# Seven block products for eight in the first product of a two-layer feed-forward kernel's second layer

## The chip, the cores and the metric

The kernel runs on one core of one Trainium2 chip, as one launch. The metric is device time in microseconds (us) of that launch. Runs of a kernel are compared by their median; a profiled execution gives a trace of every instruction on TensorE (PE; its weight loads are PEld), VectorE (DVE), ScalarE (ACT), GpSimd (POOL) and the DMA queues.

## What is computed

```python
def reference(x, filt_r, filt_i, moe_w_in, moe_w_out, moe2_w_in, moe2_w_out):
    y = irfft(rfft(x, axis=1) * (filt_r + 1j * filt_i))   # x: (2, 3008, 256) float32
    t = y.reshape(6016, 256)
    h = t @ moe_w_in                                      # (256, 2048), float64 in memory
    t = where(h > 0, h, exp(min(h, 0)) - 1) @ moe_w_out   # (2048, 256)
    h = t @ moe2_w_in
    return (h * clip(h + 3, 0, 6) / 6) @ moe2_w_out
```

A long convolution along the sequence, then two feed-forward layers, each 256 to 2048 to 256 with a nonlinearity between its two products.

## The kernel before

The convolution is done as small Fourier matrices on TensorE; it fills the first part of the launch and is interleaved with layer one. The 6016 tokens lie in 12 blocks (`BLOCKS`: 512, 512, 512, 512, 480, 480 for each half of the batch), channels on partitions, tokens along the free dimension. The 2048 inner features are 16 chunks (`NF`) of 128.

Float32 is kept by splitting every operand in a high and a low float32r part (`split`, lines 74 to 76: ScalarE rounds a copy, VectorE subtracts it) and doing three matmuls for each product (`mm3`, lines 78 to 81: high by low, low by high, high by high).

A unit `u = (layer, block, chunk)` is one chunk of inner features for one block of tokens. `g1(u)` (line 328) does its first product: two halves of 128 input channels, so six matmuls into one PSUM bank. Then the nonlinearity: in layer one ScalarE's two activations and VectorE's combination (lines 341 to 345); in layer two ScalarE's ReLU with a bias of three and VectorE's minimum-and-multiply from the same bank (lines 347 to 350). `g_split(u)` splits the result, and `g2(u)` (line 359) does the second product, another six matmuls, summed over the 16 chunks in two PSUM banks (`outs`), which are emptied at a block's last chunk. Of 8 PSUM banks the other six go round among the `g1` results.

The program's order is written out by hand (`tc.manual_schedule()`), and each engine takes its instructions in that order. At step n (lines 587 to 596) come the functions listed in `pre[n]`, then `g1` of unit n, `g_split` of unit n-1, `g2` of unit n-3 (`SKEW`), then `post[n]`. So on VectorE the order at a step is: what `pre[n]` asks of it, the combination of unit n, the low half of the split of unit n-1; and the first matmul of `g2` reads that low half two steps later. Units 0 to 191 are layer one, 192 to 383 layer two, block after block.

Layer two's weights are float64 words in memory. During units 100 to 179 `w_chain` (line 291) makes the two float32r parts of each of the 16 chunks, seven small steps for each chunk, 112 steps dealt out over 80 units: `w_words` (VectorE and ScalarE), then `w_parts` (line 273), whose last step (line 283) ends a chunk and writes it to the scratch `scrw` by SyncE's queue (line 287). Odd chunks end at units 110, 120, ..., 170 and 179. The parts are read back by GpSimd's queue (`w_load`, line 314) into the buffers of layer one's weights as these come free, from unit 179 on. Layer one's outputs stay in SBUF (`x2`, line 387) and are split for layer two by `x_split`.

Three pools matter: `p4` has 20 buffers of 4 KB per partition (tag `t4`), `p2` 20 buffers of 2 KB (tag `t2`), `ps` the 8 PSUM banks. A new tile of a tag takes the buffer that came free first in program order and waits until its last user is done.

Of the kernel before, what the change touches and what calls it, by code (L numbers as in the profile page):

```python
# [13 lines left out]
ALU = mybir.AluOpType  # L14
# [23 lines left out]
def _f32(t):  # L38
    return t.bitcast(F32)
# [3 lines left out]
def fft_conv_moe_moe2(ctx, tc, xp, fq, sg, cs1, cs1t, cs2, ci2, ci1, ident, w1i, w1o, w2i, w2o, out):  # L43
# [34 lines left out]
    def mm3(acc, wh, wl, xh, xl, start, stop):  # L78
        nc.tensor.matmul(acc, wh, xl, start=start, stop=False)  # L79
        nc.tensor.matmul(acc, wl, xh, start=False, stop=False)  # L80
        nc.tensor.matmul(acc, wh, xh, start=False, stop=stop)  # L81
# [236 lines left out]
    xs, x2, gs, outs = {}, {}, {}, {}  # L318

    def x_split(layer, blk, h):  # L320
        n = BLOCKS[blk % 6]
        src = yblk[blk // 6, blk % 6] if layer == 0 else x2[blk]
        if h == 0:
            xs[layer, blk] = t4([P, 2, 512], F32R), t4([P, 2, 512], F32R)
        hi, lo = xs[layer, blk]
        split(hi[:, h, :n], lo[:, h, :n], src[:, h, :n])

    def g1(u):
        l, blk, f = u
# [10 lines left out]
        if l == 0:  # L340
            nc.scalar.activation(r[:, :n], acc[:, :n], AF.Relu, scale=-1.0)  # L341
            nc.scalar.activation(r[:, :n], r[:, :n], AF.Exp, scale=-1.0)  # L342
            nc.vector.scalar_tensor_tensor(  # L343
                out=r[:, :n], in0=r[:, :n], scalar=-1.0, in1=acc[:, :n], op0=ALU.add, op1=ALU.max
            )
        else:
            nc.scalar.activation(r[:, :n], acc[:, :n], AF.Relu, bias=three)  # L347
            nc.vector.scalar_tensor_tensor(  # L348
                out=r[:, :n], in0=r[:, :n], scalar=6.0, in1=acc[:, :n], op0=ALU.min, op1=ALU.mult
            )  # L350
        gs[u] = r

    def g_split(u):
        n = BLOCKS[u[1] % 6]
        gh, gl = t2([P, 512], F32R), t2([P, 512], F32R)
        split(gh[:, :n], gl[:, :n], gs[u][:, :n])
        gs[u] = gh, gl

    def g2(u):
        l, blk, f = u  # L360
        n = BLOCKS[blk % 6]
        gh, gl = gs.pop(u)
# [10 lines left out]
        sc = 1.0 if l == 0 else 1.0 / 6.0  # L373
        t0 = (blk // 6) * S + EDGES[blk % 6]
        dst = out[:, t0 : t0 + n].rearrange("(c p) t -> p c t", p=P)
        nc.scalar.activation(t[:, 0, :n], o[0][:, :n], AF.Copy, scale=sc)
        if u == units[-1]:
            m = n // 2
            nc.sync.dma_start(dst[:, 0, :], t[:, 0, :n])
            nc.scalar.activation(t[:, 1, :m], o[1][:, :m], AF.Copy, scale=sc)  # L380
            nc.vector.tensor_scalar_mul(t[:, 1, m:n], o[1][:, m:n], sc)
            nc.sync.dma_start(dst[:, 1, :], t[:, 1, :n])
            return
        nc.vector.tensor_scalar_mul(t[:, 1, :n], o[1][:, :n], sc)
        del outs[l, blk]
        if l == 0:
            x2[blk] = t
        else:
            nc.sync.dma_start(dst, t[:, :, :n])
# [9 lines left out]
    def at(slots, n, fn, *args):  # L399
        slots[n].append(lambda: fn(*args))  # L400
# [116 lines left out]
    with tc.manual_schedule():  # L517
        for key, src in (("s1t", cs1t), ("id", ident), ("sg", sg), ("s2", cs2), ("i2", ci2), ("i1", ci1)):
            load_mat(key, src)
        three = const.tile([P, 1], F32, name="three")  # L520
        nc.vector.memset(three, 3.0)
        engs = (nc.scalar, nc.vector)

        warm = const.tile([P, 512], F32, name="warm")
        nc.gpsimd.memset(warm, 0.0)
        acc = bank()
        for _ in range(WARM):
            nc.tensor.matmul(acc, warm[:, :P], warm, start=True, stop=True)
# [12 lines left out]
        nsign = 2  # L541
        for step in PROLOGUE.split():
            what, h, g = step[:-2], int(step[-2]), int(step[-1])
            if what == "T":
                tr(0, h, g, nc.scalar if g > 1 else engs[g])
            elif what == "S":
                s2_mm(0, h, g)
                mult(0, h, g)
            elif what == "A":
                s1t(0, h, g, engs[g % 2])  # L550
            elif what == "I":
                i2_mm(0, h, g)
# [129 lines left out]
```

## Time and profile before

| | |
|---|---|
| median of 3 runs (lowest to highest) | 1156.41 us (1154.66 to 1157.22) |
| the profiled execution's own time | 1154.02 us |
| its span, first to last instruction | 1152.3 us |
| PE busy | 1136.1 us |
| DVE busy | 760.1 us |
| ACT busy | 695.7 us |
| POOL busy | 73.7 us |

Matmuls are pipelined and the profile models their ends, so a matmul's duration is longer than the distance from its start to the next one's start. The rate of TensorE is read from starts. ACT and DVE instructions overlap a little too: two in a row start closer together than one lasts.

### The profile page before, as it was taken

Reading aid. Unit: us, or ns where it says so; the run is one execution under the profiler, and the core shown is the slowest. Engines: PE = TensorE matmul, PEld = TensorE weight load, DVE = VectorE, ACT = ScalarE, POOL = GpSimd, SP = SyncE. Lnnn points to the kernel's source line nnn. Section 1 sums busy time; section 2 is a strip of 40 time slices with the busy share of each in tenths; the row PEclk is TensorE's granted clock in tenths of the full one; section 3 lists DMA queues with packets and bytes.
Section 4 is the critical chain, followed back from the end, with each engine's and each line's share of the span. In section 5 each row is a group of like instructions: output and inputs, shape, how many; then the busy total and the mean of one; then the engine's idle time right before and its main releaser. Section 6 shows DMA issues by size and latency. Waiting matters only on the chain.

```text
span 1152.3 us, 13760 instructions
## 1 busy us (share of the span) xinstructions
PE 1136.1 (99%) x5212; PEld 942.7 (82%) x5212; DVE 760.1 (66%) x1206; ACT 695.7 (60%) x1237; POOL 73.7 (6%) x69
## 2 busy tenths in 40 slices
PE   8899999999999999999999999999999999999998
PEld 5588888788788888888888888888888888888887
DVE  6989998679963788787875555455455555455553
ACT  3477777876676777777776444444444444444443
POOL 3600000024310000000002000000000000000000
PEclk9999999999999999999999999999999999999999
DMA  9991100354522122222226100000000000000000
GB/s 290 290 300 65 42 1 1 110 160 148 165 74 72 37 74 73 74 74 73 81 84 202 54 19 1 19 19 1 19 18 1 18 19 1 19 19 1 19 18 18
DMA packets 50019, 79.75 MB, mean 69 GB/s; under 512 B 4000, under 2 KB 32544, under 8 KB 49952
## 3 DMA queue, kind: packets, MB, share of 16 engines
q1 hardware_dynamic: 46672, 70.14, 19.1%
q0 software_dynamic: 2304, 8.39, 2.4%
q8 instruction: 41, 0.67, 0.2%
q10 hardware_dynamic: 976, 0.34, 0.1%
q14 instruction: 26, 0.21, 0.1%
HBM read 54.87 MB, written 23.99 MB: 68 GB/s over the span
## 4 chain that ended last, share of the span: by engine, by line
PE 92%; DMA 4%; DVE 2%; ACT 0%; SPq 0%; issue 0%; POOL 0%; ACTq 0%; POOLq 0%; DVEq 0%
PE ps L79 30%; PE ps L81 30%; PE ps L80 30%; PE ps L216 2%; DMA raw<-in_w1o 1%; DMA t<-in_fq 1%; DMA t<-in_xp 1%; DVE t L190 1%; DVE t L189 1%; DMA id<-in_ident 1%; POOL t L192 0%; DVE t L76 0%; DMA t<-scr 0%; PE ps L197 0%; ACT t L75 0%
## 5 line engine op out<-in xcount | busy, mean ns | idle before, releaser
L79 PE MATMUL ps<-t,w 128*128 128x512 f32 (+1 forms) x1536 | 593.6, 386 | 0.6 <-DVE t L76 0.5
L81 PE MATMUL ps<-t,w 128*128 128x512 f32 (+1 forms) x1536 | 592.2, 386 | 0.0
L80 PE MATMUL ps<-t,w 128*128 128x512 f32 (+1 forms) x1536 | 592.1, 385 | 0.0
L76 DVE TENSOR_TENSOR t<-t,t 128x512 fp32r<-128x512 f32 (+2 forms) x472 | 329.0, 705 | 9.5 <-ACT t L75 7.6
L79 PEld LDWEIGHTS ps<-t,w 128*128 128x128 f32 x1536 | 288.2, 188 | 56.9 <-PE ps L81 0.9
L81 PEld LDWEIGHTS ps<-t,w 128*128 128x128 f32 x1536 | 288.2, 188 | 55.2
L80 PEld LDWEIGHTS ps<-t,w 128*128 128x128 f32 x1536 | 288.2, 188 | 54.8
L75 ACT ACTIVATE t<-t 128x512 fp32r<-128x512 f32 (+2 forms) x472 | 283.1, 611 | 24.6 <-POOL t L192 24.1
L348 DVE SCALAR_TENSOR_TENSOR t<-t,ps 128x512 f32<-128x512 f32 (+1 forms) x192 | 130.0, 677 | 250.7 <-ACT t L347 250.7
L347 ACT ACTIVATE t<-ps,three 128x512 f32<-128x512 f32 (+1 forms) x192 | 130.6, 680 | 268.6 <-PE ps L81 268.6
L343 DVE SCALAR_TENSOR_TENSOR t<-t,ps 128x512 f32<-128x512 f32 (+1 forms) x192 | 129.5, 675 | 109.3 <-ACT t L342 108.1
L341 ACT ACTIVATE t<-ps 128x512 f32<-128x512 f32 (+1 forms) x192 | 112.3, 585 | 104.5 <-PE ps L81 104.4
L342 ACT ACTIVATE t<-t 128x512 f32<-128x512 f32 (+1 forms) x192 | 119.8, 624 | 6.1
L125 POOL TENSOR_TENSOR t<-t,sg 128x512 f32<-128x512 f32 x24 | 30.3, 1265 | 191.6 <-DMA t<-in_fq 180.7
L192 POOL TENSOR_TENSOR t<-t,t 128x512 f32<-128x512 f32 x24 | 34.9, 1454 | 73.5 <-DVE t L190 48.8
L189 DVE TENSOR_TENSOR t<-ps,t 64x512 f32<-64x512 f32 x48 | 33.1, 689 | 5.7 <-POOL t L125 2.8
L216 PEld LDWEIGHTS ps<-i,t 96*128 96x128 f32 x256 | 31.3, 192 | 3.6 <-issue 2.5
L216 PE MATMUL ps<-i,t 96*128 96x94 f32 x256 | 31.1, 273 | 0.4 <-DMA t<-scr 0.4
L316 POOL DMA_DIRECT2D w<-scrw x16 | 8.6, 540 | 298.8 <-PE ps L81 298.8
L70 ACT ACTIVATE t<-ps 128x512 f32<-128x512 f32 (+12 forms) x51 | 19.4, 421 | 12.4 <-PE ps L149 8.0
L269 DVE SCALAR_TENSOR_TENSOR t<-raw,t 128x512 f32<-128x512 uint32 x32 | 22.3, 697 | 2.0
L263 DVE SCALAR_TENSOR_TENSOR t<-raw,t 128x512 uint32<-128x512 uint32 x32 | 22.7, 710 | 0.4
(54 smaller groups left out, 384.1 us busy)
## 6 DMA issues: line engine op xcount, KB each, us to landing
t<-in_fq SPq DMA_DIRECT2D x24, 512.0 KB, 6.2
scrw<-t SPq DMA_DIRECT2D x16, 512.0 KB, 3.0
w<-scrw POOLq DMA_DIRECT2D x16, 512.0 KB, 4.5
t<-in_xp SPq DMA_DIRECT2D x16, 384.0 KB, 5.2
scr<-t SPq DMA_DIRECT2D x24, 256.0 KB, 2.7
t<-scr SPq DMA_DIRECT2D x16, 384.0 KB, 5.1
raw<-in_w1i SPq DMA_DIRECT2D x18, 256.0 KB, 5.8
raw<-in_w1o SPq DMA_DIRECT2D x18, 256.0 KB, 5.7
```

The lines of the kernel that those rows point to most:

```text
L75: nc.scalar.activation(hi, src, AF.Copy)
L76: nc.vector.tensor_tensor(out=lo, in0=src, in1=_f32(hi), op=ALU.subtract)
L79: nc.tensor.matmul(acc, wh, xl, start=start, stop=False)
L80: nc.tensor.matmul(acc, wl, xh, start=False, stop=False)
L81: nc.tensor.matmul(acc, wh, xh, start=False, stop=stop)
L189: nc.vector.tensor_tensor(out=v[o], in0=acc[a], in1=flat(f[a, 1]), op=ALU.mult)
L216: nc.tensor.matmul(accs[h, jg][:, (j - jg * TG) * TJ : (j - jg * TG + 1) * TJ], vin[b, h, j // 8][:, j % 8, :], mats["i1"], start=True, st ...
L341: nc.scalar.activation(r[:, :n], acc[:, :n], AF.Relu, scale=-1.0)
L342: nc.scalar.activation(r[:, :n], r[:, :n], AF.Exp, scale=-1.0)
L343: nc.vector.scalar_tensor_tensor(out=r[:, :n], in0=r[:, :n], scalar=-1.0, in1=acc[:, :n], op0=ALU.add, op1=ALU.max)
L347: nc.scalar.activation(r[:, :n], acc[:, :n], AF.Relu, bias=three)
L348: nc.vector.scalar_tensor_tensor(out=r[:, :n], in0=r[:, :n], scalar=6.0, in1=acc[:, :n], op0=ALU.min, op1=ALU.mult)
```

## The change

In layer two the first product is done for pairs: two chunks of inner features by two blocks of tokens, with the 256 input channels as two halves, is a 2 by 2 by 2 product of blocks, done with seven block products and sums (Winograd's form of Strassen's scheme). Six pairs of blocks by eight pairs of chunks are 48 groups (`group(p, q, old, first)`).

- For each pair of chunks four weight sums are made (`w_sums`), split, written to the scratch `scrs` and read back (`s_load`): four GpSimd operations of 128x256, one ScalarE rounding of 128x512, one GpSimd subtraction of 128x512, one VectorE addition of 128x512. `w_sums` stands in the last step of `w_parts` for odd chunks.
- Layer one's outputs go to memory (`scrx`) and are read back per pair (`x2_load`, SyncE's queue); GpSimd makes four sums of them (`x_sums`), and seven operands are split (`x_part`) in place of four.
- In a group ScalarE copies three partial products out of PSUM (`copy`) and VectorE makes three sums (`add`); the fourth partial product builds up in its bank. The second product is the same as before, for four (chunk, block) pairs of the group before (`old`), its matmuls set between the seven products (`second` is `g2`'s inner part; 24 matmuls a group). ReLU and the gate read SBUF for three of the four.
- The outputs of both blocks of a pair take four PSUM banks, emptied in the next pair's first group (`out_evac`).
- The operands of the next pair are loaded, summed and split after groups q = 2 to 7 of each pair (`ahead2`); those of the first pair at units 160 to 188.

The diff, cut to its core (`copy`, `relu`, `gate` and `second` are as `copy` of a bank to SBUF, lines 347, 348 and 369 of before):

```diff
--- before.py
+++ after.py
@@ w_parts, layer two
             nc.sync.dma_start(scrw[f], _f32(hl.rearrange("p q f -> p (q f)")))
+            halves[f] = hl
+            if f % 2:
+                w_sums(f // 2)
         yield
+    def w_sums(q):
+        e, o = (_f32(halves.pop(f)) for f in (2 * q, 2 * q + 1))
+        a11, a12, a21, a22 = e[:, :, 0:P], e[:, :, P : 2 * P], o[:, :, 0:P], o[:, :, P : 2 * P]
+        t, r = t4([P, 2, 4, P]), t4([P, 2, 4, P], F32R)
+        s1, s2, s3, s4 = (t[:, :, i, :] for i in range(4))
+        for out, a, b, op in (
+            (s1, a21, a22, ALU.add), (s2, s1, a11, ALU.subtract),
+            (s3, a11, a21, ALU.subtract), (s4, a12, s2, ALU.subtract),
+        ):
+            nc.gpsimd.tensor_tensor(out=out, in0=a, in1=b, op=op)
+        th, tl, rh, rl = (x.rearrange("p i f -> p (i f)") for x in (t[:, 0], t[:, 1], r[:, 0], r[:, 1]))
+        nc.scalar.activation(rh, th, AF.Copy)
+        nc.gpsimd.tensor_tensor(out=th, in0=th, in1=_f32(rh), op=ALU.subtract)
+        nc.vector.tensor_tensor(out=rl, in0=th, in1=tl, op=ALU.add)
+        nc.sync.dma_start(scrs[q], _f32(r.rearrange("p q i f -> p (q i f)")))
...
+    def s_load(q):
+        if q < 3:
+            if q == 0:
+                sums["z"] = p12.tile([P, 3, 2, 4, P], F32R, tag="zt", name=name("zt"))
+            sums[q] = sums["z"][:, q]
+        else:
+            sums[q] = t4([P, 2, 4, P], F32R)
+        nc.gpsimd.dma_start(sums[q].rearrange("p q i f -> p (q i f)"), scrs[q])
...
@@ g2, end of a block of layer one
+        nc.scalar.activation(t[:, 0, :n], o[0][:, :n], AF.Copy)
+        nc.vector.tensor_copy(t[:, 1, :n], o[1][:, :n])
+        del outs[l, blk]
+        nc.sync.dma_start(scrx[blk][:, :, :n], t[:, :, :n])
...
+    def x_sums(p, i):
+        n = BLOCKS[2 * p % 6]
+        if i == 0:
+            xt[p] = [t2([P, 512]) for _ in range(4)]
+        b11, b21 = (xb[p, 0][:, c, :n] for c in range(2))
+        b12, b22 = (xb[p, 1][:, c, :n] for c in range(2))
+        t1, t2_, t3, t4_ = (t[:, :n] for t in xt[p])
+        out, a, b = ((t1, b12, b11), (t2_, b22, t1), (t3, b22, b12), (t4_, b21, t2_))[i]
+        nc.gpsimd.tensor_tensor(out=out, in0=a, in1=b, op=ALU.subtract)
+
+    def x_part(p, m):
+        n = BLOCKS[2 * p % 6]
+        src = {
+            1: xb[p, 0][:, 0], 2: xb[p, 0][:, 1], 3: xb[p, 1][:, 1],
+            4: xt[p][3], 5: xt[p][0], 6: xt[p][1], 7: xt[p][2],
+        }[m][:, :n]
+        ops[p, m] = t4([P, 2, 512], F32R)
+        split(ops[p, m][:, 0, :n], ops[p, m][:, 1, :n], src)
+    def prod(p, q, m, acc, start):
+        n = BLOCKS[2 * p % 6]
+        if m in (1, 2):
+            w = wts[1, 2 * q][:, :, (m - 1) * P : m * P]
+        elif m == 4:
+            w = wts[1, 2 * q + 1][:, :, P : 2 * P]
+        else:
+            w = sums[q][:, :, {5: 0, 6: 1, 7: 2, 3: 3}[m], :]
+        x = ops[p, m]
+        mm3(acc[:, :n], w[:, 0], w[:, 1], x[:, 0, :n], x[:, 1, :n], start, True, True)
...
+    def out_evac(p, k):
+        for d in range(2):
+            o, t = outs.pop((p, k, d)), t2([P, 512])
+            if d == 0:
+                nc.scalar.activation(t[:, :n], o[:, :n], AF.Copy, scale=1.0 / 6.0)
+            else:
+                nc.vector.tensor_scalar_mul(t[:, :n], o[:, :n], 1.0 / 6.0)
+            nc.sync.dma_start(out[d * P : (d + 1) * P, t0 : t0 + n], t[:, :n])
+
...
+        def add(self, key, u, bank_):
+            n = self.n
+            self.h[key] = t2([P, 512])
+            nc.vector.tensor_tensor(out=self.h[key][:, :n], in0=bank_[:, :n], in1=u[:, :n], op=ALU.add)
+        def part(self, key):
+            n, g = self.n, self.g[key]
+            gh, gl = t2([P, 512], F32R), t2([P, 512], F32R)
+            split(gh[:, :n], gl[:, :n], g[:, :n])
+            self.g[key] = gh, gl
...
+    def group(p, q, old, first):
+        g = Group(p, q)
+        a, b, c = bank(), bank(), bank()
+        prod(p, q, 1, a, True)
+        m1 = g.copy(a)
+        prod(p, q, 2, b, True)
+        g.add((0, 0), m1, b)
+        if old:
+            old.part((1, 0))
+            old.relu((0, 1))
+            old.gate((0, 1))
+            old.second((0, 0))
+        else:
+            first[0]()
+        g.relu((0, 0))
+        if old:
+            old.part((0, 1))
+        g.gate((0, 0))
+        prod(p, q, 6, a, False)
+        u2 = g.copy(a)
+        prod(p, q, 5, c, True)
+        g.part((0, 0))
+        if old:
+            old.second((1, 1))
+        else:
+            first[1]()
+        prod(p, q, 7, a, False)
+        u3 = g.copy(a)
+        g.add((1, 1), u3, c)
+        if old:
+            old.second((1, 0))
+            if old.q == NF // 2 - 1:
+                out_evac(old.p, 0)
+        else:
+            first[2]()
+        g.relu((1, 1))
+        g.gate((1, 1))
+        if old:
+            old.second((0, 1), (0,))
+        prod(p, q, 4, a, False)
+        g.h[1, 0] = a
+        g.relu((1, 0))
+        g.gate((1, 0))
+        if old:
+            old.second((0, 1), (1,))
+            if old.q == NF // 2 - 1:
+                out_evac(old.p, 1)
+        g.part((1, 1))
+        prod(p, q, 3, c, False)
+        g.add((0, 1), u2, c)
+        return g
...
-    units += [(1, blk, f) for blk in range(12) for f in range(NF)]
+    for q in range(NF // 2):
+        at(post, 172 + q, s_load, q)
+    for n, fn, i in ((160, x2_load, 0), (161, x2_load, 1), (166, x_sums, 0), (167, x_sums, 1), (168, x_sums, 2),
+                     (169, x_sums, 3), (176, x_part, 1), (178, x_part, 2), (180, x_part, 6), (182, x_part, 5),
+                     (184, x_part, 7), (186, x_part, 4), (188, x_part, 3)):
+        at(pre, n, fn, 0, i)
...
+        ahead2 = {2: [(x2_load, 0)], 3: [(x2_load, 1), (x_sums, 0)], 4: [(x_sums, 1), (x_sums, 2)],
+                  5: [(x_sums, 3), (x_part, 1)], 6: [(x_part, 2), (x_part, 6)],
+                  7: [(x_part, 5), (x_part, 7), (x_part, 4), (x_part, 3)]}
+        for p in range(6):
+            for q in range(NF // 2):
+                old = group(p, q, old, [rest(NU + i) for i in range(3)])
+                for fn, i in ahead2.get(q, ()) if p < 5 else ():
+                    fn(p + 1, i)
+        old.part((1, 0))
...
```

## Rows read from the trace of the kernel before

**Rows 1.** The page, busy time of each engine, and TensorE's granted clock in 40 slices of the span (9 is full speed).

```profile
PE 1136.1 (99%) x5212; PEld 942.7 (82%) x5212; DVE 760.1 (66%) x1206; ACT 695.7 (60%) x1237; POOL 73.7 (6%) x69
...
PEclk9999999999999999999999999999999999999999
```

**Rows 2.** The page, the chain of work that ended last, shares of the span by line.

```profile
PE ps L79 30%; PE ps L81 30%; PE ps L80 30%; PE ps L216 2%; DMA raw<-in_w1o 1%; DMA t<-in_fq 1%; DMA t<-in_xp 1%; DVE t L190 1%; DVE t L189 1%; DMA id<-in_ident 1%; POOL t L192 0%; DVE t L76 0%; DMA t<-scr 0%; PE ps L197 0%; ACT t L75 0%
```

**Rows 3.** Busy time by stretch: start and end, length, then for each engine us busy (and instructions), TensorE's granted clock, DMA share and GB/s. The first stretch is layer one while layer two's weights are made, the second is layer two.

```profile
420.00:500.00 80.00, 80.00 (x355) 66.24 (x354) 63.73 (x106) 59.86 (x106) 0.00 (x0) 1.00 0.24 79
800.00:900.00 100.00, 100.00 (x460) 85.86 (x459) 51.41 (x84) 48.03 (x84) 0.00 (x0) 1.00 0.04 16
```

**Rows 4.** Timeline of TensorE in layer two: start, length, instruction. 800.46 begins a first product of 512 tokens, 801.82 the second product that follows it, 803.18 the next first product, of 480 tokens, 804.48 the second product after that.

```profile
800.46 0.39 PE L79 MATMUL ps<-t,w 128*128 128x512 f32 x1
...
801.82 0.39 PE L79 MATMUL ps<-t,w 128*128 128x512 f32 x1
...
803.18 0.38 PE L79 MATMUL ps<-t,w 128*128 128x480 f32 x1
...
804.48 0.39 PE L79 MATMUL ps<-t,w 128*128 128x512 f32 x1
```

**Rows 5.** Groups of instructions of the whole run with shapes kept apart: how many, us busy, mean ns of one, idle time before them and what ended it.

```profile
L76 DVE TENSOR_TENSOR t<-t,t 128x512 fp32r<-128x512 f32 x312 | 219.0, 707 | 4.1 <-ACT t L75 3.8
L75 ACT ACTIVATE t<-t 128x512 fp32r<-128x512 f32 x312 | 191.3, 620 | 24.1 <-POOL t L192 24.1
L347 ACT ACTIVATE t<-ps,three 128x512 f32<-128x512 f32 x128 | 88.3, 690 | 180.5 <-PE ps L81 180.5
L348 DVE SCALAR_TENSOR_TENSOR t<-t,ps 128x512 f32<-128x512 f32 x128 | 88.2, 689 | 168.1 <-ACT t L347 168.1
...
L190 DVE TENSOR_TENSOR t<-ps,t 128x512 f32<-128x512 f32 x24 | 16.6, 692 | 0.5
...
L203 ACT ACTIVATE t<-ps 128x512 f32<-128x512 f32 x24 | 14.2, 591 | 13.0 <-PE ps L197 12.5 <-PE ps L81 0.6
```

**Rows 6.** Timeline of ScalarE in layer two: ReLU of a unit and the split of the unit before it.

```profile
802.02 0.69 ACT L347 ACTIVATE t<-ps,three 128x512 f32<-128x512 f32 x1 [1.51 <-PE ps L81]
802.60 0.62 ACT L75 ACTIVATE t<-t 128x512 fp32r<-128x512 f32 x1
```

**Rows 7.** Timeline of VectorE in layer two: the gate and the low half of the split.

```profile
802.74 0.69 DVE L348 SCALAR_TENSOR_TENSOR t<-t,ps 128x512 f32<-128x512 f32 x1 [1.43 <-ACT t L347]
803.35 0.69 DVE L76 TENSOR_TENSOR t<-t,t 128x512 fp32r<-128x512 f32 x1
```

**Rows 8.** Timeline of VectorE in layer one at unit 120, an odd chunk's last step (L283), the combination of unit 120, and the low half of the split of unit 119.

```profile
439.16 0.69 DVE L283 TENSOR_TENSOR t<-t,t 128x512 fp32r<-128x512 f32 x1
439.95 0.69 DVE L343 SCALAR_TENSOR_TENSOR t<-t,ps 128x512 f32<-128x512 f32 x1
440.56 0.69 DVE L76 TENSOR_TENSOR t<-t,t 128x512 fp32r<-128x512 f32 x1
```

**Rows 9.** Timeline of ScalarE at the same place: the first activations of units 120 and 122 (that of 121 lies between).

```profile
438.66 0.60 ACT L341 ACTIVATE t<-ps 128x512 f32<-128x512 f32 x1 [0.94 <-PE ps L81]
...
444.10 0.60 ACT L341 ACTIVATE t<-ps 128x512 f32<-128x512 f32 x1 [0.94 <-PE ps L81]
```

**Rows 10.** The instructions of line 283: count, shortest, median and longest ns, first and last start in us. These are layer two's weights.

```profile
L283 DVE TENSOR_TENSOR t<-t,t x16: 682/691/694, 398.4 to 597.3; 128x512 fp32r<-128x512 f32 x16
```

**Rows 11.** The chain of work between 290 and 296 us: a hand-over from VectorE to GpSimd to ScalarE.

```profile
291.65 0.70 DVE t L190
...
292.60 1.50 POOL t L192
...
294.12 0.63 ACT t L75
```

**Rows 12.** GpSimd's two-input operation of line 192 in the stretch 18 to 30 us.

```profile
L192 POOL TENSOR_TENSOR t<-t,t x4: 1267/1269/1274, 18.8 to 27.9; 128x512 f32<-128x512 f32 x4
```

**Rows 13.** The same line in the stretch 60 to 340 us.

```profile
L192 POOL TENSOR_TENSOR t<-t,t x12: 1279/1546/1622, 249.8 to 329.5; 128x512 f32<-128x512 f32 x12
```

**Rows 14.** GpSimd's multiplication of line 125 by a sign that is read broadcast, whole run.

```profile
L125 POOL TENSOR_TENSOR t<-t,sg x24: 1035/1336/1492, 12.2 to 316.1; 128x512 f32<-128x512 f32 x24
```

**Rows 15.** Timeline of VectorE at 278 to 282 us.

```profile
278.30 0.68 DVE L76 TENSOR_TENSOR t<-t,t 128x512 fp32r<-128x512 f32 x1
278.90 0.65 DVE L343 SCALAR_TENSOR_TENSOR t<-t,ps 128x480 f32<-128x480 f32 x1
279.46 1.18 DVE L76 TENSOR_TENSOR t<-t,t 128x480 fp32r<-128x480 f32 x1
280.82 1.27 DVE L76 TENSOR_TENSOR t<-t,t 128x512 fp32r<-128x512 f32 x1 [0.18 <-ACT t L75]
```

**Rows 16.** Timeline of GpSimd in the same stretch.

```profile
278.55 1.57 POOL L192 TENSOR_TENSOR t<-t,t 128x512 f32<-128x512 f32 x1 [3.99 <-DVE t L190]
280.08 1.45 POOL L125 TENSOR_TENSOR t<-t,sg 128x512 f32<-128x512 f32 x1
```

**Rows 17.** Timeline of all engines at the end of the run.

```profile
1147.52 0.38 PE L81 MATMUL ps<-t,w 128*128 128x480 f32 x1
...
1148.34 0.41 DVE L381 TENSOR_SCALAR t<-ps 128x240 f32<-128x240 f32 x1 [2.93 <-ACT t L380]
1148.77 0.34 SPq L382 DMA_DIRECT2D out<-t  x1
```

More of the change, by code (lines that the diff above doesn't have):

```diff
@@ L76, in split, with mm3 @@
         nc.vector.tensor_tensor(out=lo, in0=src, in1=_f32(hi), op=ALU.subtract)
[L78 to L81, printed above, removed]
+    def mm3(acc, wh, wl, xh, xl, start, stop, more=False):
+        nc.tensor.matmul(acc, wh, xl, start=start, stop=False, skip_group_check=more)
+        nc.tensor.matmul(acc, wl, xh, start=False, stop=False, skip_group_check=more)
+        nc.tensor.matmul(acc, wh, xh, start=False, stop=stop, skip_group_check=more)
     def flat(t):
@@ L287, in w_parts @@
             nc.sync.dma_start(scrw[f], _f32(hl.rearrange("p q f -> p (q f)")))
+            halves[f] = hl
+            if f % 2:
+                w_sums(f // 2)
         yield
+    halves = {}
+    scrs = dram.tile([NF // 2, P, 1024], F32, name="scrs")
+    def w_sums(q):
[13 more added lines that the diff above has]
+        nc.sync.dma_start(scrs[q], _f32(r.rearrange("p q i f -> p (q i f)")))
     def w_chain(layer, first, last, fetch):
@@ L316, in w_load @@
         nc.gpsimd.dma_start(wts[1, f].rearrange("p q f -> p (q f)"), scrw[f])
-    xs, x2, gs, outs = {}, {}, {}, {}
+    sums = {}
+    def s_load(q):
[6 more added lines that the diff above has]
+        nc.gpsimd.dma_start(sums[q].rearrange("p q i f -> p (q i f)"), scrs[q])
+    xs, gs, outs = {}, {}, {}
+    scrx = [dram.tile([P, 2, 512], F32, name=f"scrx_{i}") for i in range(12)]
     def x_split(layer, blk, h):
         n = BLOCKS[blk % 6]
-        src = yblk[blk // 6, blk % 6] if layer == 0 else x2[blk]
+        src = yblk[blk // 6, blk % 6]
         if h == 0:
@@ L339, in g1 @@
         r = t2([P, 512])
[L340 to L350, printed above, removed]
+        nc.scalar.activation(r[:, :n], acc[:, :n], AF.Relu, scale=-1.0)
+        nc.scalar.activation(r[:, :n], r[:, :n], AF.Exp, scale=-1.0)
+        nc.vector.scalar_tensor_tensor(
+            out=r[:, :n], in0=r[:, :n], scalar=-1.0, in1=acc[:, :n], op0=ALU.add, op1=ALU.max
+        )
         gs[u] = r
@@ L372, in g2 @@
         t = t4([P, 2, 512])
-        sc = 1.0 if l == 0 else 1.0 / 6.0
-        t0 = (blk // 6) * S + EDGES[blk % 6]
[L375 to L387, printed above, removed]
-        else:
-            nc.sync.dma_start(dst, t[:, :, :n])
+        nc.scalar.activation(t[:, 0, :n], o[0][:, :n], AF.Copy)
+        nc.vector.tensor_copy(t[:, 1, :n], o[1][:, :n])
+        del outs[l, blk]
+        nc.sync.dma_start(scrx[blk][:, :, :n], t[:, :, :n])
+    xb, xt, ops, prev = {}, {}, {}, []
+    def x2_load(p, k):
+        n = BLOCKS[(2 * p + k) % 6]
+        xb[p, k] = t4([P, 2, 512])
+        nc.sync.dma_start(xb[p, k][:, :, :n], scrx[2 * p + k][:, :, :n])
@@ new lines, in prod, with second @@
+    def prod(p, q, m, acc, start):
[8 more added lines that the diff above has]
+        mm3(acc[:, :n], w[:, 0], w[:, 1], x[:, 0, :n], x[:, 1, :n], start, True, True)
+    def second(p, q, i, k, d, g):
+        n = BLOCKS[2 * p % 6]
+        if (p, k, d) not in outs:
+            outs[p, k, d] = bank()
+        w = wts[1, 2 * q + i]
+        s = slice(256 + d * P, 256 + (d + 1) * P)
+        mm3(
+            outs[p, k, d][:, :n], w[:, 0, s], w[:, 1, s], g[0][:, :n], g[1][:, :n],
+            q == 0 and i == k, q == NF // 2 - 1 and i != k,
+        )
@@ new lines, in out_evac, with __init__, copy, relu @@
+    def out_evac(p, k):
+        blk = 2 * p + k
+        n = BLOCKS[blk % 6]
+        t0 = (blk // 6) * S + EDGES[blk % 6]
+        for d in range(2):
[5 more added lines that the diff above has]
+            nc.sync.dma_start(out[d * P : (d + 1) * P, t0 : t0 + n], t[:, :n])
+    class Group:
+        def __init__(self, p, q):
+            self.p, self.q, self.n = p, q, BLOCKS[2 * p % 6]
+            self.h, self.g = {}, {}
+        def copy(self, bank_):
+            t = t2([P, 512])
+            nc.scalar.activation(t[:, : self.n], bank_[:, : self.n], AF.Copy)
+            return t
+        def add(self, key, u, bank_):
+            n = self.n
+            self.h[key] = t2([P, 512])
+            nc.vector.tensor_tensor(out=self.h[key][:, :n], in0=bank_[:, :n], in1=u[:, :n], op=ALU.add)
+        def relu(self, key):
+            self.g[key] = t2([P, 512])
+            nc.scalar.activation(self.g[key][:, : self.n], self.h[key][:, : self.n], AF.Relu, bias=three)
+        def gate(self, key):
+            n, r = self.n, self.g[key]
+            nc.vector.scalar_tensor_tensor(
+                out=r[:, :n], in0=r[:, :n], scalar=6.0, in1=self.h.pop(key)[:, :n], op0=ALU.min, op1=ALU.mult
+            )
+        def part(self, key):
[3 more added lines that the diff above has]
+            self.g[key] = gh, gl
+        def second(self, key, d=(0, 1)):
+            for d_ in d:
+                second(self.p, self.q, key[0], key[1], d_, self.g[key])
@@ L585, in fft_conv_moe_moe2 @@
                 split_mat("s1")
+        NU = len(units)
         for n, u in enumerate(units):
@@ L596, in fft_conv_moe_moe2, with rest, run @@
                 fn()
-        g_split(units[-1])
-        for u in units[-SKEW:]:
-            g2(u)
+        def rest(n):
+            def run():
+                if n == NU:
+                    g_split(units[-1])
+                g2(units[n - SKEW])
+                for fn in post[n]:
+                    fn()
+            return run
+        old = None
+        ahead2 = {2: [(x2_load, 0)], 3: [(x2_load, 1), (x_sums, 0)], 4: [(x_sums, 1), (x_sums, 2)],
[7 more added lines that the diff above has]
+        old.part((1, 0))
+        old.relu((0, 1))
+        old.gate((0, 1))
+        old.second((0, 0))
+        old.part((0, 1))
+        old.second((1, 1))
+        old.second((1, 0))
+        out_evac(old.p, 0)
+        old.second((0, 1))
+        out_evac(old.p, 1)
 def _tables():
```

## The prediction

> **What bounds the kernel now.** I read the page first: TensorE is busy 99% of the span at full granted clock [rows 1], and the chain that ended last is nine tenths the three matmul lines [rows 2]. Then the stretches: in layer one, while layer two's weights are made, VectorE is busy 63.73 of 80 us and ScalarE 59.86; in layer two 51.41 and 48.03 of 100 [rows 3]. So TensorE sets the time in both layers, with less room beside it in layer one. A busy TensorE is modelled, so its rate is read from starts: twelve matmuls of 512 tokens take 803.18 - 800.46 = 2.72 us, 0.227 each; six of 480 take 804.48 - 803.18 = 1.30, 0.217 each [rows 4]. A gain in layer two is a gain in matmuls, unless another engine comes late.
>
> The other engines' prices: a split is 0.62 us on ScalarE and 0.69 on VectorE, a ReLU 0.69, a gate 0.69; a sum with one PSUM operand is like line 190, 0.69, a copy out of PSUM like line 203, 0.59 [rows 5]. In a row they start closer together: 0.58 on ScalarE after a ReLU (the spacing of its length less 0.1, so 0.5 after a copy or split), 0.61 on VectorE [rows 6, 7]. ScalarE to VectorE costs 0.03 us (802.71 to 802.74) [rows 6, 7]. The ReLU starts 0.20 us after the start of the matmul behind its own last one (801.82 to 802.02) [rows 4, 6].
>
> **What is removed.** Each of the 48 groups has 21 first-product matmuls for 24; the second product keeps its 24. 32 groups have 512 tokens, 16 have 480: 32 x 3 x 0.227 + 16 x 3 x 0.217 = 32.1 us. This is certain as work; what follows is what becomes of it.
>
> **What is added in layer one: `w_sums`, eight times.** Its price is a wait, since each engine keeps its order. Behind an odd chunk's last step VectorE's next instruction is the final addition, which needs GpSimd's subtraction, which needs ScalarE's rounding, which needs all four GpSimd sums. ScalarE's rounding stands before the first activation of the unit at hand, VectorE's addition before that unit's combination and before the low half of the split of the unit before. Take unit 120. The chunk's last step ends at 439.16 + 0.69 = 439.85, and now the combination follows at 439.95 and the low half of unit 119 ends at 441.25 [rows 8]. Unit 122's activation starts at 444.10, so TensorE had ended that product at 443.90 [rows 9] and then wants the low half of 119: 2.65 us to spare.
>
> Line 283 has one length in all 16 places [rows 10], so unit 120 stands for the eight.
>
> With the change: VectorE to GpSimd 0.25 us (292.35 to 292.60), GpSimd to ScalarE 0.02 [rows 11]; ScalarE to GpSimd is in no such row, I take the 0.25. A two-input GpSimd operation of 512 elements is 1.27 us with VectorE quiet [rows 12], 1.55 with VectorE at work [rows 13]; VectorE is held up here, so 1.27. None of 256 elements is shown. Its bounds are half of the shortest 512 one, 0.52 [rows 14], and the whole 1.27; I take 0.70, near the lower end, since elements make most of the length. Then: 439.85 + 0.25 + 4 x 0.70 = 442.90; rounding 0.02 + 0.62, 443.54; subtraction 0.25 + 1.27, 445.06; addition from 445.09; the combination at 445.70, the low half from 446.31 to 447.00. TensorE wanted it at 443.90: 3.1 us late. Eight times: 25 us. With 0.52 each stall is 2.4 (19 us), with 1.27 it is 5.4 (43 us). Behind the stall VectorE has a backlog, but gains about 0.6 us a unit (2.72 less two instructions of a unit and 1.4 weight steps at 0.61), so it has caught up before the next chunk pair, ten units on.
>
> At nothing: the writes of sums and of layer one's outputs and their reading back. SyncE's queue waits some 6 us at each of the eight sums, with the next raw weights behind it, but these are fetched a chunk, five units or 13.6 us, ahead. GpSimd's queue holds the first `w_load` behind the last sums; if that cover went, layer two's start would be late by the few us of one read. The seven splits of the first pair stand in units with room.
>
> **What is added in layer two, within a group.** ScalarE has 11 instructions a group (3 copies, 4 ReLUs, 4 splits) and VectorE 11 (3 sums, 4 gates, 4 low halves): 11 x 0.55 = 6.1 and 11 x 0.61 = 6.7 us of the group's 45 x 0.227 = 10.2. Both fit; the order decides. I set the times from the group's first matmul, 0.68 us a product. Copy of M1 at 0.88; its sum on VectorE 1.56; the low half of the group before 2.17, its gate 2.78 to 3.47; that one's split on ScalarE 3.50 to 4.12; copy of U2 4.02 to 4.61. TensorE wants this bank again at 5.44: 0.8 to spare. The copy of U3 ends at 6.91 and is wanted at 8.16; the sum from the third bank ends at 7.63, wanted at 9.53. The group's last sum runs 0.8 us into the next group, in front of the sum at 1.56, and delays nothing. So a plain group has no stall.
>
> **At the end of each pair of blocks** (five times) the next pair's splits are queued before the next group's instructions: one after q = 5, two after q = 6, four after q = 7. Four low halves on VectorE, 0.61 apart from 1.38 on, put the first sum at 3.82, the gate at 5.04 to 5.73, the split at 5.76 to 6.38, the U2 copy at 6.28 to 6.87: TensorE is 1.5 us late. With two it is late by 0.3, with one early. 5 x 1.8 = 9 us. If the two engines took these splits in gaps it would be 0; if the emptying of the four output banks, in the same group, falls in the way as well, some 15.
>
> **GpSimd's four `x_sums` a pair** (the first pair's lie in layer one). Beside a GpSimd operation VectorE's two-SBUF-input low half lasts 1.18 us, not 0.65, and 1.27, not 0.68, while a combination with a PSUM operand stays at 0.65 [rows 15, 16]: 0.55 us for each GpSimd operation, 2.2 a pair. Of this 0.8 is spare in a group, so 1.4 a pair if all fall in one group, nothing if in two; I take 0.5, five times 2.5 us, ends 0 and 7. The Trainium skill, page "SBUF — State Buffer", section "Who interferes with whom", says more: that the port pair of the two engines is an exclusive lock and the later one fully blocks. The rows show a delay of a third of the GpSimd operation; the rule is a rival below.
>
> **The end.** The last group's leftovers are eight products of TensorE, no more than it would have done in place; their last split comes 0.3 us late by the same spacing. Behind the last matmul one output of 0.69 on VectorE replaces two halves in a row (1147.90 to 1148.75 [rows 17]): -0.1. Together 0.2.
>
> **Sum.** Against the profiled execution, 1154.0: - 32.1 + 25 + 9 + 2.5 + 0.2 = 1158.6. The median of the runs is 2.4 above that execution, so 1161.
>
> **Rivals.** First, layer two keeps its saving: ScalarE and VectorE take the pair's splits and sums without being late, which they do from 2.3 us of spare at the U2 copy on, where I find 0.8. For it speaks that both are about half idle there [rows 3]; against it, that the chain of five hand-overs, not their load, makes the time. It gives 1161 - 11.5 = 1149.5, and 1143.5 with the short sums: faster. Second, GpSimd's operations of 256 elements cost as much as those of 512: 43 for 25, 1179. For it speaks that a short instruction may be mostly overhead; against it, that none is shown. Third, a GpSimd operation holds VectorE up for its whole length: 4 x 1.4 - 0.8 = 4.8 us a pair, 24 for 2.5, 1182. Against it stand the 1.18 and 1.27 [rows 15]. By the lock of the page named above, it would be this one.
>
> **How the numbers follow.** Forecast 0.48, first rival 0.30, second 0.15, third 0.07. From 1144 (first rival, short sums) to 1179 (second) holds eight in ten. A measurement of this kernel tells about 0.2%, 2.3 us. Faster by more is most of the first rival and the forecast's lowest part, 0.26 + 0.06; within it the rest of the first rival and the forecast with short sums, 0.04 + 0.13; slower the rest, 0.51.
>
> **What would show it.** Layer one: around units 110 to 179 eight gaps on TensorE of some 3 us, ended by VectorE's line 76, with ScalarE idle on GpSimd before them; the units between them at 2.72 us. Without these gaps the main step is wrong. GpSimd's 128x256 operations at 0.70 us. Layer two: 45 matmuls in 10.2 us a group, a gap of 1.5 us in the first group of each pair but the first, ended by ScalarE's copy. VectorE's low halves at 1.2 us beside `x_sums`, 0.69 elsewhere. A group that stalls without splits of the next pair would mean that my order of hand-overs is wrong, and would count 48 times.

## The result and the profile after

The changed kernel takes 1170.39 us (median), the kernel before beside it 1156.82: ratio 1.0115, 95% interval 1.0092 to 1.0137, so slower by 1.15%. One of its four runs, 1187.60 us at a mean granted clock of 0.971, was a slow one and is left out of the ratio. The prediction was 1161, range 1144 to 1179. The profiled execution took 1169.87 us; its span is 1168.0.

The page of the changed kernel, busy time and granted clock:

```profile
PE 1120.7 (96%) x5068; PEld 921.3 (79%) x5068; DVE 873.2 (75%) x1376; ACT 791.6 (68%) x1406; POOL 145.0 (12%) x141
...
PEclk9999999999999999899998999999999999999999
```

Against [rows 1]: 144 matmuls fewer, as counted, and TensorE no longer busy for 99% of the span. Two of the 40 slices have a granted clock below 0.9 of full (a 9 stands for 0.9 and more). What TensorE waited for, all from one answer (engine, line and releaser; us in total, times, longest):

```profile
PE ps L79 <- DVE t L76: 26.0, 13, 3.6
PE ps L79 <- ACT t L476: 5.7, 5, 1.2
```

Lines 79 and 76 are the first matmul of a product and the low half of a split; line 476 is the copy out of PSUM in a group. The same answer for the kernel before has 1.6 us for the first of these waits (3 times, longest 0.9) and none for the second. Two places, then: layer one, and the ends of the pairs.

**Layer one.** GpSimd, ScalarE, VectorE and TensorE at the chunk that ends with unit 120 (timeline of each engine):

```profile
446.37 0.74 POOL L307 TENSOR_TENSOR t<-t 128x256 f32<-128x256 f32 x1 [25.45 <-DVE t L283]
447.18 2.13 POOL L307 TENSOR_TENSOR t<-t,t 128x256 f32<-128x256 f32 x3
450.05 1.27 POOL L310 TENSOR_TENSOR t<-t,t 128x512 f32<-128x512 f32 x1 [0.74 <-ACT t L309]
```

```profile
449.35 0.63 ACT L309 ACTIVATE t<-t 128x512 fp32r<-128x512 f32 x1 [5.25 <-POOL t L307]
449.88 0.58 ACT L376 ACTIVATE t<-ps 128x512 f32<-128x512 f32 x1
```

```profile
451.36 0.69 DVE L311 TENSOR_TENSOR t<-t 128x512 fp32r<-128x512 f32 x1 [5.13 <-POOL t L310]
451.97 0.68 DVE L378 SCALAR_TENSOR_TENSOR t<-t,ps 128x512 f32<-128x512 f32 x1
452.56 0.68 DVE L76 TENSOR_TENSOR t<-t,t 128x512 fp32r<-128x512 f32 x1
```

```profile
453.30 0.50 PE L79 MATMUL ps<-t,w 128*128 128x512 f32 x1 [2.87 <-DVE t L76]
453.64 0.39 PE L80 MATMUL ps<-t,w 128*128 128x512 f32 x1
```

Read down: GpSimd's sums 446.37 to 449.31, ScalarE standing 5.25 us in front of its rounding, VectorE 5.13 in front of its addition, and ScalarE's first activation of unit 120 (L376) queued behind a rounding it has nothing to do with. TensorE starts the second product 3.03 us later than its own rate would have it. The eight places, by starts of matmuls beyond 0.227 (or 0.217) us: 3.29, 3.03, 3.02, 3.72, 3.02, 3.20, 3.20, 3.05, together 25.5 us. Why the first and the fourth are longer was not worked out.

**The clock.** Behind four of the eight the matmuls come at another rate. TensorE at the third (timeline):

```profile
483.66 0.80 PE L79 MATMUL ps<-t,w 128*128 128x512 f32 x1 [2.86 <-DVE t L76]
484.25 0.63 PE L80 MATMUL ps<-t,w 128*128 128x512 f32 x1
484.68 0.63 PE L81 MATMUL ps<-t,w 128*128 128x512 f32 x1
...
489.37 0.57 PE L80 MATMUL ps<-t,w 128*128 128x512 f32 x1
489.78 0.39 PE L81 MATMUL ps<-t,w 128*128 128x512 f32 x1
490.01 0.40 PE L79 MATMUL ps<-t,w 128*128 128x512 f32 x1
```

0.43 us from start to start in place of 0.23, for 14 matmuls. The four stretches by window (start:end, length, busy time of PE, PEld, DVE, ACT, POOL with counts, granted clock, DMA share, GB/s), and one behind a gap where it did not happen:

```profile
483.66:489.78 6.12, 6.12 (x15) 4.79 (x15) 4.91 (x9) 3.93 (x7) 0.00 (x0) 0.50 0.65 231
518.00:520.40 2.40, 2.40 (x7) 1.82 (x7) 2.30 (x6) 2.26 (x5) 0.00 (x0) 0.50 0.94 304
609.30:612.60 3.30, 3.30 (x9) 2.77 (x9) 3.27 (x7) 3.27 (x7) 1.14 (x3) 0.50 1.00 322
637.50:643.30 5.80, 5.80 (x15) 4.78 (x15) 3.08 (x6) 3.07 (x7) 1.58 (x3) 0.50 0.50 160
452.00:460.00 8.00, 6.70 (x29) 5.55 (x30) 7.90 (x15) 7.29 (x14) 0.00 (x0) 1.00 0.38 131
```

In these four stretches the granted clock is 0.50 of full, 1.2 GHz for 2.4, while matmuls run. Their starts beyond the full rate: 2.94 + 1.37 + 1.67 + 2.92 = 8.9 us.

**The ends of the pairs.** ScalarE, VectorE and TensorE at the end of the first pair (timelines):

```profile
747.40 2.70 ACT L75 ACTIVATE t<-t 128x512 fp32r<-128x512 f32 x5
750.00 0.58 ACT L476 ACTIVATE t<-ps 128x512 f32<-128x512 f32 x1
...
753.66 0.63 ACT L75 ACTIVATE t<-t 128x512 fp32r<-128x512 f32 x1 [0.47 <-DVE t L490]
754.20 0.58 ACT L476 ACTIVATE t<-ps 128x512 f32<-128x512 f32 x1
```

```profile
749.34 2.48 DVE L76 TENSOR_TENSOR t<-t,t 128x512 fp32r<-128x512 f32 x4
751.75 0.68 DVE L482 TENSOR_TENSOR t<-ps,t 128x512 f32<-128x512 f32 x1
...
752.95 0.68 DVE L490 SCALAR_TENSOR_TENSOR t<-t,t 128x512 f32<-128x512 f32 x1
```

```profile
754.83 0.50 PE L79 MATMUL ps<-t,zt 128*128 128x512 f32 x1 [1.14 <-ACT t L476]
755.16 0.40 PE L80 MATMUL ps<-t,zt 128*128 128x512 f32 x1
```

VectorE's four low halves in a row (749.34 to 751.82), then the first sum (L482), the gate (L490, ends 753.63), ScalarE's split, the copy of U2 (the second of a group's three copies, line 476; it ends at 754.78), and TensorE 1.3 us late: the chain as worked out. In a plain group the same copy ends 0.77 us before TensorE takes the bank (701.18 to 701.94, for one). With the smaller delay one group earlier and the slow first start behind each, the five ends lose 1.90, 1.81, 1.89, 1.91 and 1.77, together 9.3 us; the end of the run 0.5.

**The account.** -32.1 + 25.5 + 8.9 + 9.3 + 0.5 = +12.1 against 1168.0 - 1152.3 = 15.7 between the two profiled spans. Of the other 3.6, 2.8 lies before 96 us, where the programs are the same and executions differ as much: the matmul that starts at 95.9 us before starts at 98.7 after, 97.2 in e1 and 102.6 in e2 (below). Part of it is the clock there too, 0.50 from 39.2 to 42.6 us in the changed kernel's execution; in e2's it is 0.50 from 52.4 to 72.9 us. The rest is in small delays. The medians differ by 13.6.

### The profile page after: what moved, and what is told of

The parts are those of the page before. It is cut to its first block, busy times and chain, and to the rows that moved or that the text cites. A ratio compares the mean times of both kernels' runs of the same rounds, so it can differ in the third digit from the quotient of the medians.

```text
span 1168.0 us, 14327 instructions
## 1 busy us (share of the span) xinstructions
PE 1120.7 (96%) x5068; PEld 921.3 (79%) x5068; DVE 873.2 (75%) x1376; ACT 791.6 (68%) x1406; POOL 145.0 (12%) x141
## 4 chain that ended last, share of the span: by engine, by line
PE 77%; DVE 10%; ACT 3%; POOL 3%; issue 3%; DMA 3%; SPq 0%; ACTq 0%; POOLq 0%; DVEq 0%
PE ps L79 25%; PE ps L81 25%; PE ps L80 25%; DVE t L76 4%; PE ps L216 2%; POOL t L307 2%; DVE t L378 1%; DVE t L189 1%; DVE t L490 1%; DVE t L482 1%; DMA t<-in_fq 1%; DMA t<-in_xp 1%; POOL t L310 1%; ACT t L75 1%; DVE t L190 1%
## 5 line engine op out<-in xcount | busy, mean ns | idle before, releaser
L79 PE MATMUL ps<-t,w 128*128 128x512 f32 (+1 forms) x1296 | 506.0, 390 | 25.0 <-DVE t L76 24.8
L80 PE MATMUL ps<-t,w 128*128 128x512 f32 (+1 forms) x1296 | 503.3, 388 | 0.0
L81 PE MATMUL ps<-t,w 128*128 128x512 f32 (+1 forms) x1296 | 502.9, 388 | 0.0
L79 PEld LDWEIGHTS ps<-t,w 128*128 128x128 f32 x1296 | 245.5, 189 | 77.1 <-DVE t L76 28.1
L81 PEld LDWEIGHTS ps<-t,w 128*128 128x128 f32 x1296 | 245.3, 189 | 47.5
L80 PEld LDWEIGHTS ps<-t,w 128*128 128x128 f32 x1296 | 245.4, 189 | 46.8
L378 DVE SCALAR_TENSOR_TENSOR t<-t,ps 128x512 f32<-128x512 f32 (+1 forms) x192 | 129.2, 673 | 94.7 <-ACT t L377 93.8
L376 ACT ACTIVATE t<-ps 128x512 f32<-128x512 f32 (+1 forms) x192 | 111.8, 582 | 91.6 <-PE ps L81 91.4
L486 ACT ACTIVATE t<-t,three 128x512 f32<-128x512 f32 (+1 forms) x144 | 99.3, 710 | 48.1 <-DVE t L482 47.0
L490 DVE SCALAR_TENSOR_TENSOR t<-t,t 128x512 f32<-128x512 f32 (+1 forms) x144 | 97.2, 675 | 34.4 <-ACT t L486 34.4
L476 ACT ACTIVATE t<-ps 128x512 f32<-128x512 f32 (+1 forms) x144 | 83.4, 579 | 29.7 <-PE ps L81 25.1
L482 DVE TENSOR_TENSOR t<-ps,t 128x512 f32<-128x512 f32 (+1 forms) x144 | 96.5, 673 | 6.4 <-ACT t L476 3.8
L424 POOL TENSOR_TENSOR t<-t,t 128x512 f32<-128x512 f32 (+1 forms) x18 | 25.0, 1390 | 360.2 <-PE ps L81 298.6
L79 PE MATMUL ps<-t,t 128*128 128x512 f32 (+1 forms) x120 | 46.8, 390 | 0.5
L490 DVE SCALAR_TENSOR_TENSOR t<-t,ps 128x512 f32<-128x512 f32 (+1 forms) x48 | 32.5, 678 | 18.4 <-ACT t L486 18.0
L81 PE MATMUL ps<-t,t 128*128 128x512 f32 (+1 forms) x120 | 46.3, 386 | 0.0
L80 PE MATMUL ps<-t,t 128*128 128x512 f32 (+1 forms) x120 | 46.3, 386 | 0.0
L486 ACT ACTIVATE t<-ps,three 128x512 f32<-128x512 f32 (+1 forms) x48 | 32.6, 680 | 18.4 <-PE ps L81 18.0
```

The lines of the kernel that those rows point to most:

```text
L79: nc.tensor.matmul(acc, wh, xl, start=start, stop=False, skip_group_check=more)
L80: nc.tensor.matmul(acc, wl, xh, start=False, stop=False, skip_group_check=more)
L81: nc.tensor.matmul(acc, wh, xh, start=False, stop=stop, skip_group_check=more)
L378: nc.vector.scalar_tensor_tensor(out=r[:, :n], in0=r[:, :n], scalar=-1.0, in1=acc[:, :n], op0=ALU.add, op1=ALU.max)
L476: nc.scalar.activation(t[:, : self.n], bank_[:, : self.n], AF.Copy)
L482: nc.vector.tensor_tensor(out=self.h[key][:, :n], in0=bank_[:, :n], in1=u[:, :n], op=ALU.add)
```

## The experiments

All ratios are to the kernel before on the same chip (1154.4 us in the first four, 1155.0 in the last three), so 0.001 is 1.2 us.

| run | median us | ratio, 95% interval |
|---|---|---|
| e1_late_sums | 1135.29 | 0.9835 (0.9821 to 0.9850) |
| e2_no_sums | 1133.76 | 0.9816 (0.9798 to 0.9833) |
| e3_filled_gaps | 1160.52 | 1.0052 (1.0037 to 1.0067) |
| e4_one_split | 1161.96 | 1.0070 (1.0046 to 1.0094) |
| e5_after_again | 1168.84 | 1.0118 (1.0084 to 1.0152) |
| e6_vector_sums | 1142.32 | 0.9877 (0.9825 to 0.9928) |
| e7_late_and_spread | 1125.04 | 0.9723 (0.9679 to 0.9768) |

**e1_late_sums**

```diff
+        half[q] = t, r
...
+    def w_round(q):
...
         nc.scalar.activation(rh, th, AF.Copy)
         nc.gpsimd.tensor_tensor(out=th, in0=th, in1=_f32(rh), op=ALU.subtract)
+
+    def w_last(q):
...
         nc.vector.tensor_tensor(out=rl, in0=th, in1=tl, op=ALU.add)
         nc.sync.dma_start(scrs[q], _f32(r.rearrange("p q i f -> p (q i f)")))
...
-        at(post, 172 + q, s_load, q)
+        at(post, 172 + q if q < 7 else 184, s_load, q)
+        n = 110 + 10 * q if q < 7 else 179
+        at(pre, n + 2, w_round, q)
+        at(pre, n + 4, w_last, q)
```

> The eight chains of weight sums are kept, but their links stand apart in the written order: ScalarE's rounding and GpSimd's subtraction two units after GpSimd's sums, VectorE's addition four units after them. Theory (the wait): the eight gaps of 3.0 to 3.7 us on TensorE come from ScalarE and VectorE standing in front of work that is ready; they go, and with them the four stretches at half clock (8.9 us): 1170.4 - 25.5 - 8.9 = 1136 us, granted clock 1.0 throughout layer one. Rival (the load): the added work itself is too much for VectorE in layer one (27.9 us asked of it for 27.2 us of matmuls in ten units, and GpSimd in its way): gaps remain in front of the second products, at least half of the 34 us stays, 1153 us or more.

0.9835, or 1135 us: 32.3 us less than 1.0115 x 1154.4 = 1167.7, expected 34. The same instructions, none left out. TensorE's waits are now:

```profile
PE ps L79 <- ACT t L486: 5.7, 5, 1.2
...
PE ps L79 <- DVE t L76: 2.3, 6, 0.8
```

The 26.0 us behind line 76 are 2.3, the granted clock is full in every slice of layer one, and the pair ends (line 486 is the copy here) are as before. The load theory falls, though GpSimd now works beside VectorE and does stretch it: at the same chunk GpSimd's last three sums take 2.92 us here for 2.13 above, and VectorE's instructions with two SBUF inputs last up to 1.23 us beside the sums and 1.60 beside the subtraction, for 0.69. It costs VectorE, which had room, and not TensorE: the one gap of 0.5 us left in layer one (567.4) stands behind a low half that lasted 1.40 us beside an operation of `x_sums`.

**e2_no_sums**

```diff
-            halves[f] = hl
-            if f % 2:
-                w_sums(f // 2)
...
-        nc.gpsimd.dma_start(sums[q].rearrange("p q i f -> p (q i f)"), scrs[q])
+        nc.gpsimd.dma_start(sums[q].rearrange("p q i f -> p (q i f)"), scrw[2 * q])
```

> Leaves the weight sums out altogether: layer two reads one chunk's weight parts in their place, so its numbers are not the reference's; every matmul of layer two is still done. Both theories: no gaps of 3 us in layer one, 1136 us. It is the floor for the run with the late links: by the wait theory the two agree within 3 us, by the load theory this one is faster by 17 us or more.

0.9816: 2.2 us below e1, within the 3 us. So the sums' work itself is nearly hidden; its place in the order was the cost.

**e3_filled_gaps**

```diff
+        again = 2 if u in filled else 0
-        for c in range(2):
+        for c in [0, 1] * (1 + again):
...
+        filled = [units[112 + 10 * q if q < 7 else 181] for q in range(8)]
```

> The changed kernel with twelve matmuls more at each of the eight gaps (the first product of the unit ahead of the gap is done three times over, 2.7 us, inside the 3.0 to 3.7 us that TensorE stands still). Theory: the half clock follows from TensorE standing still; with the gap filled the clock stays at full level, 1170.4 - 8.9 = 1161.5 us, and the eight waits themselves stay. Rival: the half clock has another cause (the stretch of work before, or chance between executions): the four stretches stay, 1170 us. If the added matmuls don't lie in the gaps, they add up to 8 x 2.7 = 22 us.

1.0052, 7.3 us less than the changed kernel's ratio gives, with 96 matmuls more. In its trace the second products behind the first three gaps start as far apart as before (422.22, 452.61 and 482.99 us, against 422.90, 453.30 and 483.66), still by VectorE's line 76; TensorE runs up to all eight but for 0.3 to 1.0 us, and no matmul of layer one behind them is at half rate:

```profile
482.20 0.39 PE L80 MATMUL ps<-t,w 128*128 128x512 f32 x1
482.43 0.39 PE L81 MATMUL ps<-t,w 128*128 128x512 f32 x1
482.99 0.50 PE L79 MATMUL ps<-t,w 128*128 128x512 f32 x1 [0.17 <-DVE t L76]
483.32 0.40 PE L80 MATMUL ps<-t,w 128*128 128x512 f32 x1
```

So at these places the half clock follows from TensorE standing still, and is a cost of its own beside the wait: 8.9 us in the account, 7.3 here (the intervals of the two ratios do not touch, and the mean granted clock of e3's four runs is 0.996 to 1.000, of the unfilled kernel's nine in e5 0.981 to 0.991).

**e4_one_split**

```diff
+        ahead2 = {0: [(x2_load, 0), (x2_load, 1)], 1: [(x_sums, 0), (x_part, 1)], 2: [(x_part, 2), (x_sums, 1)],
+                  3: [(x_part, 3), (x_sums, 2)], 4: [(x_part, 5), (x_sums, 3)], 5: [(x_part, 6)],
+                  6: [(x_part, 7)], 7: [(x_part, 4)]}
```

> The splits of the next pair's seven operands are spread, one after each of the groups 1 to 7, with loads and sums earlier; nothing else changes. Theory (order of work at the end of a pair): the gaps of 1.4 and 0.3 us in the first and last groups of each pair, 8.8 us in all five, go: 1161.6 us. Rival (VectorE's and ScalarE's load in layer two, and GpSimd's sums beside them): the splits cost the same wherever they stand, 0.3 us for each or more, and the time stays within 3 us of 1170.4.

1.0070, 5 us less than the changed kernel's ratio gives; the two intervals touch, so the trace is the better witness. Layer two has no gap over 0.4 us left, and its matmul starts lose 2.3 us where the changed kernel's lose 9.8; but the clock fell behind five of layer one's gaps, 9.8 us, not 8.9. The order theory holds for the pair ends, with 7.5 of the 8.8 us. The rest are five new delays of 0.2 to 0.3 us (0.1 more behind each) in groups beside GpSimd's sums for the next pair.

**e5_after_again**

> The changed kernel once more, as it is, beside the next two on their chip. Both theories: 1.15% above the kernel before, eight gaps of 3.0 to 3.7 us in layer one, half clock behind some of them.

1.0118. The gaps in layer one are the same to 0.02 us; half clock came behind five of them (10.0 us).

**e6_vector_sums**

```diff
-            nc.gpsimd.tensor_tensor(out=out, in0=a, in1=b, op=op)
+            nc.vector.tensor_tensor(out=out, in0=a, in1=b, op=op)
-        nc.gpsimd.tensor_tensor(out=th, in0=th, in1=_f32(rh), op=ALU.subtract)
+        nc.vector.tensor_tensor(out=th, in0=th, in1=_f32(rh), op=ALU.subtract)
```

> The weight sums stand where the change put them, but VectorE does GpSimd's part: four 128x256 sums of about 0.4 us and the subtraction of 0.69. Wait theory: the chain from the chunk's last step to the low half that TensorE wants shrinks by GpSimd's slower work and the hand-overs, 4 x (0.74 - 0.36) + (1.27 - 0.61) + 2 x 0.2 = 2.6 us, so gaps of 3.1 us become 0.5 us, too short for the clock to fall: 25.5 + 8.9 - 8 x 0.5 = 30 us less than the changed kernel, 0.988 of the kernel before. Load theory: VectorE then has 2.1 us more to do in each ten units in which it already lacks time, so the gaps shrink by less than half, 1.00 of the kernel before or more.

0.9877. The chain on VectorE (timeline), unit 110:

```profile
412.52 0.69 DVE L283 TENSOR_TENSOR t<-t,t 128x512 fp32r<-128x512 f32 x1
413.25 0.42 DVE L307 TENSOR_TENSOR t<-t 128x256 f32<-128x256 f32 x1
413.71 1.09 DVE L307 TENSOR_TENSOR t<-t,t 128x256 f32<-128x256 f32 x3
415.50 0.69 DVE L310 TENSOR_TENSOR t<-t,t 128x512 f32<-128x512 f32 x1 [0.70 <-ACT t L309]
416.23 0.69 DVE L311 TENSOR_TENSOR t<-t 128x512 fp32r<-128x512 f32 x1
```

The gaps are 0.9 to 1.5 us, 8.5 in all, not 4: the wait for ScalarE's rounding (0.70) stays in VectorE's queue. No half clock. Work taken on by the busier engine made the kernel 26.5 us faster than the changed kernel beside it (1142.3 against 1168.8), which the load theory excludes.

**e7_late_and_spread**

e1 and e4 together.

> The late links of the weight sums and the one-by-one splits of the next pair together. If the two costs are separate: e1's 0.9835 of the kernel before less 8.8 us, 0.976 (1127 us where before is 1154.4), against 1154.4 - 32.1 = 1122 for the saving whole. Rival: what is no longer late at a pair's end turns up elsewhere in layer two (buffers, GpSimd's sums beside VectorE), 0.98 or more.

0.9723, 1125 us: faster than both kernels. No gap over 0.4 us is left in either layer; against 1155.0 - 32.1 = 1122.9 for the saving whole, 2.1 us are missing.

## Why the prediction was right

**Matmuls removed:** 144 counted and 144 gone, 32.1 us; e7 collects nearly all of it.

**`w_sums`, 25 us:** 25.5, by the mechanism named. The 128x256 operation on GpSimd, bounded by 0.52 and 1.27 and taken as 0.70, measured 0.74. The units behind each gap ran at full rate where the clock did, as the backlog was reckoned. That the place of the chain in the order is the cause is shown by e1 (the same work, links apart) and e6 (more work for VectorE, a shorter chain).

**Pair ends, 9 us:** 9.3. Four splits cost 1.3 (1.5 expected), two 0.2 to 0.3 (0.3), one nothing.

**`x_sums`, 2.5 us:** no gap, within the ends 0 and 7. Three low halves in each pair are stretched by 0.3 to 0.6 us beside GpSimd's sums, but they stand behind the U2 copy: during the first pair, with the sums between 700.2 and 723.9 us, that copy keeps its 0.77 us of spare in all three groups. So their place made them free. In e4, where the sums stand in other groups, gates are stretched too, and TensorE is late five times. The reading of [rows 15, 16] as a share of the GpSimd operation was wrong, though: both long instructions there end 0.52 and 0.56 us after GpSimd's (280.12 and 281.53). In e7 a gate with two SBUF inputs shows it once more (VectorE, then GpSimd):

```profile
654.69 1.78 DVE L500 SCALAR_TENSOR_TENSOR t<-t,t 128x512 f32<-128x512 f32 x1
```

```profile
654.33 1.60 POOL L434 TENSOR_TENSOR t<-t,t 128x512 f32<-128x512 f32 x1 [5.88 <-PE ps L79]
```

GpSimd ends at 655.93, the gate 0.54 later. All such instructions of two SBUF inputs that start under a GpSimd operation and last over 0.9 us, 42 in the changed kernel behind 96 us, end 0.52 to 0.55 us after it. So VectorE waits out the rest of GpSimd's operation and then does its work. The Trainium skill, page "SBUF — State Buffer", section "Who interferes with whom", calls the port pair that the two engines share an exclusive lock; the trace agrees, with the 0.54 above. The third rival had this rule right and its price wrong: an instruction loses only what is left of the GpSimd operation, and only three of a pair's four sums met one.

**The step that was missing** is the clock: the sum took matmuls after a gap at full rate, since the profiled execution of the kernel before shows full clock throughout [rows 1], and it had no gap of 3 us to show otherwise. That term, 0 in the sum, measured 8.9. The sum gave +4.6 us and the spans show +15.7. Of the 11.1 between them the clock is 8.9, the 3.6 of the account that no term has come next, and the three terms that were there came out 1.1 larger; the 2.5 of `x_sums` that did not come stands against them. That 1170 still lies in the range is in part luck: the range reached up to 1179 for long GpSimd operations, which did not come, and not for the clock. The Trainium skill, page "TensorE: Matmul & The Clock Gate", section "HAM oscillation — how this bites in real kernels", tells that a wait of TensorE in the middle of a kernel can throttle it and that the work behind then starts at the low rate. The trace agrees (0.50 behind four of the eight gaps), and the prediction should have weighed it.

The first rival (layer two keeps its saving) needed 2.3 us of spare at the U2 copy; there were 0.77 and it fell. The second needed GpSimd's short operations at 1.27 and fell with 0.74.

## What to carry to other kernels

An instruction that is put into several engines' fixed queues costs what stands behind it while it waits: add up the whole chain from its first input to its last link, and compare it with how far each engine is ahead of the one that sets the time. If it is longer, set the links apart in the order by as much as each one takes (e1: the same instructions, 32 us less), before looking for a faster engine (e6: 26.5 us). Where a wait would stop TensorE for some us, count the rate after it too.

## What had not been expected of the hardware

Gaps of 3.0 to 3.7 us in front of a matmul, in a layer where TensorE otherwise does not stand, were followed by a granted clock of 0.50 in 4 of 8 places of one execution (for 2.4 to 6.1 us in the windows above) and in 5 of 8 of two others (e4, e5). The same place, 3.29 us in front of the first, shows it in e4 and e5 and not in the changed kernel's first execution. Gaps up to 1.5 us in the two layers (e6, e3, the pair ends) were followed by it in none.

The first 60 us, where TensorE waits often, shows that 3 us is no lower bound. Every profiled execution has one wait of 2.5 us there (TensorE's line 149 for VectorE's line 72, at about 35 us). With it the clock fell to 0.50 in the changed kernel (39.2 to 42.6 us), e1, e4 and e5, and not in the kernel before, e2, e3, e6 and e7; in e2, e3 and e5 it fell at 52 to 54 us, behind a wait of 1.4. The kernel before does not always keep its clock either: of its sixteen runs beside e5 to e7 four took 1161 to 1171 us at a mean granted clock of 0.982 to 0.993, with no trace kept.

What decides between two equal gaps stays open. The Trainium skill, page "TensorE: Matmul & The Clock Gate", section "Part 1: The HAM clock gate (the "warmup" mystery)", has the chip look at activity in windows that run freely; where a gap falls in them would then be chance. No run here shows that.
